# An attention, routing and expert kernel: the last 768 tokens of the routing moved into six blocks

## The chip, the cores and the metric

The kernel runs on one core of one Trainium2 chip. The metric is the device time of one execution in microseconds (us), as the median of several runs. The profiled execution is one more run, with a trace of every engine.

## The reference

Three stages follow each other: an attention with local windows and block sums, a mixture of 8 experts with a greedy assignment, and a dense layer pair. The change lies in the second. Its reference, cut to what matters:

```python
def _moe_ref(x, w_gate, w1, w2):          # x: 1536 x 512, w1: 8 x 512 x 1024, w2: 8 x 1024 x 512
    cap = N // E                          # 192
    flat = (x @ w_gate).flatten()
    for idx in np.argsort(-flat):         # greatest logit first
        tok, e = idx // E, idx % E
        if assigned[tok] >= 0 or counts[e] >= cap:
            continue
        assigned[tok] = e
        counts[e] += 1
    for e in range(E):
        out[assigned == e] = np.maximum(x[assigned == e] @ w1[e], 0.0) @ w2[e]
```

The last stage is `h = x @ w_in; r = max(h, 0); out = (r * r) @ w_out`, with 2048 hidden columns.

## The kernel before

**Routing in phases.** The 1536 tokens stand as 12 blocks (NBLK) of 128 in the tile `L9`, 128 partitions by 12 blocks by 9: eight logits, and a ninth column that is a floor. One phase finds the expert that is full first, closes it and takes its 192 tokens out. A phase has these steps, all in `Route` and in `routing()` inside `moe`:

- `top` (L508) takes each token's greatest open logit `m`, `choice` (L514 to L522) its expert as a one-hot `o` (the tiles `O32`) and, on GpSimd, its complement `no`.
- `row` (L534, L537) turns `m` into one row of 1536 values on every partition: 12 transposes on TensorE, three copies on ScalarE. `quarters` (L554) lays a copy out for the comparison below.
- `ge` (L570) compares, on VectorE, the whole row with each block's `m`: twelve tiles `G` of 128 x 1536, bf16. `count` (L582) multiplies them with the one-hots on TensorE, 32 rows of the result at a time, four products of 384 columns for a block of tokens, and so gets each token's rank within its expert. `cand` (L591, L593) turns the ranks into the threshold.
- A transposition (L761) and a chain of small VectorE instructions give the expert `ei` and the threshold `th`. Two products with a triangle and with ones (L799, L800) number the selected tokens; L803 to L829 mark the dead ones in `L9`.
- `t_hot` (L847 to L853), `t_idx` (L861, one small product for a block), `t_spread` (L870) and `t_sum` (L879, L880, with the casts L888 to L893) make a list of the 192 token numbers; `t_gather` (L905, L907) lets GpSimd issue two indirect DMAs, `xa` and `xb`, that fetch their rows of x.

Phase 0 stands in the attention stage by a table of its own. Phases 1 to 7 run beside the experts.

**Experts.** `x_t` (L957, L959) transposes the gathered rows, `expert` (L976, L993) does 64 matmuls of 128x128 by 192 columns in float32 for each expert. Weights come through SyncE's queue (`w_load`, L945) into eight buffers, two experts' worth.

**What sets the order.** `routing()` and `expert()` are generators. A loop at the end of `moe` keeps a clock of estimates (`T.p`, `T.v`, `T.a` for TensorE, VectorE, ScalarE) and appends to the program, at each turn, whichever of routing, the transposes of a gather or the next expert matmul can start first by that clock. A `yield t` says that the step behind it is ready at t. The order of each engine is so fixed when the program is built, and an instruction whose input is late holds up all behind it on its engine. Matmuls of an expert fill TensorE between routing's steps. `conv_idle` puts steps of the last stage's weight conversion (L647 to L657, from tiles `raw`) where VectorE is idle by that clock.

Two lines decide where a phase's index list is made:

```python
late = ph > 3                      # L720: the list of phase ph - 1 is made after this phase's row
now = ph < 3 or ph >= E - 2        # L822: the list of phase ph is made at once
```

So the lists of phases 3 to 5 are made inside the next phase.

**Last stage.** `hmm` (L1083) and `omm` (L1110) are float32r matmuls with 512 columns from about 312 us on.

Of the kernel before, what the change touches and what calls it, by code (L numbers as in the profile page):

```python
# [446 lines left out]
class Route:  # L447


    def __init__(self, tc, nc, L9, identf):  # L450
        self.tc, self.nc, self.L9, self.identf = tc, nc, L9, identf
        self.ctx = ExitStack()
        self.started, self.cnt, self.ng = set(), None, 0

    def open(self):
        nc, L9 = self.nc, self.L9
        rp = self.rp = self.ctx.enter_context(self.tc.tile_pool(name="m_r", bufs=1, side="right", reuse_waits="tile"))
        ii = rp.tile([128, 128], I32, name="ii")
        fi = rp.tile([128, 128], F32, name="fi")
# [4 lines left out]
        ji = rp.tile([128, 128], I32, name="ii")  # L464
# [33 lines left out]
    def new(self, ph):  # L498
        rp = self.rp
        self.m = rp.tile([128, NBLK], F32, name="m", bufs=2)  # L500
        self.eq = rp.tile([128, NBLK, E + 1], F32, name="eq")
        self.mw = rp.tile([128, NBLK], F32, name="mw")
        self.no = rp.tile([128, NBLK, E], F32, name="no")
        self.o = self.O32[ph % 2]

    def top(self, b0=0, b1=NBLK):

        self.nc.vector.reduce_max(self.m[:, b0:b1], self.L9[:, b0:b1], axis=AX.X)  # L508

    def choice(self, b0=0, b1=NBLK, onehot=True):  # L510

        nc, b = self.nc, slice(b0, b1)
# [36 lines left out]
    def quarters(self, b0, b1):  # L549
        nc = self.nc  # L550
        for g in range(b0 // 3, (b1 + 2) // 3):
# [25 lines left out]
    def count(self, pieces, last=False):  # L577

        for n, (c, j0, j1, t) in enumerate(pieces):
            for g in range(j0 // 3, (j1 + 2) // 3):  # L580
                lo, hi = max(j0, 3 * g), min(j1, 3 * g + 3)
                self.nc.tensor.matmul(self.cnt[32 * g:32 * g + 32, 128 * (lo - 3 * g):128 * (hi - 3 * g)],  # L582
                                      self.o[:, c, :], t[:, 128 * (lo - j0):128 * (hi - j0)],
# [4 lines left out]
    def cand(self):  # L588

        nc = self.nc  # L590
        nc.vector.scalar_tensor_tensor(self.mg, self.cnt, -(CAP - 0.5) * CS, self.mg, op0=OP.add, op1=OP.min)  # L591
        self.tm = self.rp.tile([128, 1], F32, name="tm")
        nc.vector.reduce_max(self.tm, self.mg, axis=AX.X)  # L593


def moe(tc, nc, R0, x_dram, m_dram, L9, w1, w2, win, wout, out, identf, identb, dbg=None):
# [101 lines left out]
    def routing():  # L698
        tm_at = T.v(0.1)
        for ph in range(E):  # L700
            d = st[ph] = {}
            ei = rp.tile([128, 8], U32, name="ei", bufs=4)
            es = rp.tile([128, 1], F32, name="es")
            if ph > 0:
                R0.new(ph)
                R0.top()
                m_at = T.v(0.33)
# [11 lines left out]
            if 0 < ph < E - 1:  # L719
                late = ph > 3  # L720
# [3 lines left out]
                R0.row(0, NBLK, ms4)  # L724
                row_at = T.a(1.6, T.p(1.3, m_at))
# [5 lines left out]
                G = R0.ge(0, NBLK)  # L731
                pend, ats = [], []

                def more(n):
                    while len(ats) < min(n, NBLK):
                        pend.extend(next(G))
                        ats.append(T.v(1.0, row_at))

                more(1)
                R0.quarters(0, NBLK)  # L740
# [6 lines left out]
                more(NG)  # L747
                c = 0
                for n in (2,) * 6 if ph == 1 else (4,) * 3:
                    c += n  # L750
                    yield ats[c - 1] + 0.1
                    R0.count(pend[c - n:c], c == NBLK)
                    T.p(0.3 + 0.165 * n, ats[c - 1] + 0.1)
# [32 lines left out]
            os_ = rp.tile([128, NBLK], F32, name="os")  # L786
            nc.vector.tensor_scalar(os_, mw, es, None, op0=OP.is_equal)
            sel = rp.tile([128, 2, NBLK], BF, name="sel")
# [10 lines left out]
            nc.tensor.matmul(ps[:, 0:24], low, s2, start=True, stop=True, skip_group_check=True)  # L799
            nc.tensor.matmul(ps[:, 24:48], ones, s2, start=True, stop=True, skip_group_check=True)  # L800
            T.p(0.07, sel_at + 0.1)
            sc = rp.tile([128, 24], F32, name="sc")
            nc.vector.tensor_tensor_scan(sc, ps[:, 24:48], zero24, 0.0, op0=OP.add, op1=OP.add)  # L803
# [384 lines left out]
```

## Time and profile before

| | us |
|---|---|
| median of 3 runs (580.49 to 580.98) | 580.73 |
| profiled execution, whole | 581.22 |
| its span, first to last instruction | 579.0 |
| TensorE (PE) busy in the span | 565.8 |
| VectorE (DVE) busy | 343.7 |
| ScalarE (ACT) busy | 197.0 |
| GpSimd (POOL) busy | 78.6 |

The page gives each engine's busy time, the span in 40 slices, the queues, the chain of work that ended last and the costliest groups of instructions. The views of the trace go closer: windows give busy times of a stretch, the chain gives pieces in order of time with what each added, the timeline gives each engine's instructions with start and duration, waits say who waited for whom. A duration is that of one instruction from start to its end; neighbours on an engine overlap, so a price in a stream is the distance between starts. A float32 matmul has two records.

### The profile page before, as it was taken

To read this page: it belongs to the slowest core of one execution; us is meant where nothing else is said; L and a number is where in the kernel's file an instruction comes from. 1 tells how busy PE (TensorE), PEld (TensorE's weight loads), DVE (VectorE), ACT (ScalarE), POOL (GpSimd) and SP (SyncE) were. 2 spreads that over 40 slices of the span, in tenths; PEclk is the share of its full clock that TensorE was granted. 3 is DMA by queue.
4 is the path that set the end of the run, shared out by engine and by line. 5 is a ranking of instruction groups with operands and counts; after the bars stand their busy time and mean duration, and the time that the engine had idled before them with its cause. 6 is when DMAs were issued, how large, how long until landed. Compare 5 with 4: busy or idle time off the path is not lost.

```text
span 579.0 us, 10522 instructions
## 1 busy us (share of the span) xinstructions
PE 565.8 (98%) x4131; PEld 473.7 (82%) x4131; DVE 343.7 (59%) x773; ACT 197.0 (34%) x421; POOL 78.6 (14%) x136
## 2 busy tenths in 40 slices
PE   6999998999999999999999999999999999999995
PEld 4778873698998989899999888888888888888884
DVE  6885688877879688765664987833222223222222
ACT  4887871331413313132232433423212213212221
POOL 6564400210202042020000000000300000300002
PEclk9999999999999999999999999999999999999998
DMA  9997223646544545869742443400100000100001
GB/s 225 244 198 148 93 76 121 227 144 219 199 173 143 196 143 203 291 220 402 248 157 84 145 146 109 146 0 2 72 2 0 1 0 1 72 1 0 1 0 72
DMA packets 55392, 71.33 MB, mean 123 GB/s; under 512 B 21296, under 2 KB 32560, under 8 KB 55344
## 3 DMA queue, kind: packets, MB, share of 16 engines
q1 hardware_dynamic: 53360, 64.38, 35.6%
q0 software_dynamic: 1984, 6.29, 3.2%
q8 instruction: 32, 0.52, 0.4%
q14 instruction: 16, 0.13, 0.1%
HBM read 64.37 MB, written 6.29 MB: 122 GB/s over the span
## 4 chain that ended last, share of the span: by engine, by line
PE 78%; issue 14%; DVE 3%; DMA 2%; POOL 1%; SPq 1%; ACT 1%; POOLq 0%; DVEq 0%; ACTq 0%
PE pg L1083 16%; PE ph L976 15%; PE ph L993 15%; PE ph L1110 11%; PE px L1110 4%; PE O L284 2%; PE cnt L582 2%; PE T L270 2%; DMA rawq<-in_q_dram 2%; DVE G L570 2%; PE S L250 2%; POOL out_dram L1123 1%; PE ms L534 1%; PE T L193 1%; PE T L321 1%
## 5 line engine op out<-in xcount | busy, mean ns | idle before, releaser
L976 PE MATMUL ph<-xt,w 128*128 128x192 f32 x512 | 90.6, 330 | 0.0
L570 DVE TENSOR_SCALAR G<-mrow,m 128x1536 bf16<-128x1536 f32 (+4 forms) x108 | 84.7, 837 | 8.1 <-ACT mrow L537 4.8
L993 PE MATMUL ph<-ht,w 128*128 128x192 f32 x512 | 89.3, 329 | 0.0
L993 PEld LDWEIGHTS ph<-ht,w 128*128 128x128 f32 x512 | 82.9, 190 | 2.9 <-issue 2.5
L976 PEld LDWEIGHTS ph<-xt,w 128*128 128x128 f32 x512 | 82.5, 190 | 2.8 <-issue 2.1
L1083 PE MATMUL pg<-yhi,w 128*128 128x512 f32 x192 | 59.1, 389 | 0.0
L1087 DVE TENSOR_TENSOR xa<-xa 128x512 f32<-128x512 f32 x24 | 16.6, 691 | 60.1 <-ACT xa L1086 60.0
L1087 DVE TENSOR_TENSOR xb<-xb 128x512 f32<-128x512 f32 x24 | 16.6, 691 | 59.6 <-ACT xb L1086 59.6
L1123 POOL DMA_INDIRECT out_dram<-f,sci x6 | 5.9, 978 | 300.7 <-DVE f L1121 300.0
L1083 PEld LDWEIGHTS pg<-yhi,w 128*128 128x128 f32 x192 | 36.0, 188 | 7.5
L981 ACT ACTIVATE ht<-ph 128x384 f32<-128x384 f32 x32 | 15.7, 490 | 65.3 <-PE ph L976 61.6
L1083 PE MATMUL pg<-ylo,w 128*128 128x512 f32 x96 | 37.3, 389 | 0.0
L1086 ACT ACTIVATE xb<-pg 128x512 f32<-128x512 f32 x24 | 14.3, 596 | 65.7 <-PE pg L1083 65.7
L1086 ACT ACTIVATE xa<-pg 128x512 f32<-128x512 f32 x24 | 14.3, 596 | 63.5 <-PE pg L1083 63.5
L1110 PE MATMUL ph<-w,xt 128*128 128x512 f32 x144 | 35.2, 389 | 0.0
L1110 PEld LDWEIGHTS ph<-w,xt 128*128 128x128 f32 x144 | 27.0, 188 | 5.6
L1083 PE MATMUL pg<-yhi,w2a 128*128 128x512 f32 x96 | 29.7, 391 | 0.0
L1083 PE MATMUL pg<-yhi,w2b 128*128 128x512 f32 x96 | 29.6, 389 | 0.0
L999 ACT ACTIVATE yhi<-ph 128x384 fp32r<-128x384 f32 x16 | 7.8, 491 | 58.4 <-PE ph L993 58.4
L263 ACT ACTIVATE P<-S,nm 128x120 f32<-128x120 f32 x96 | 26.6, 373 | 2.3 <-DVE nm L259 2.2
L905 POOL DMA_INDIRECT xa<-x_dram,sci x8 | 10.8, 1356 | 87.2 <-DVE sci L893 65.3
L1083 PEld LDWEIGHTS pg<-yhi,w2b 128*128 128x128 f32 x96 | 18.0, 188 | 3.8
(245 smaller groups left out, 982.4 us busy)
## 6 DMA issues: line engine op xcount, KB each, us to landing
w<-in_moe_w_dram SPq DMA_DIRECT2D x64, 512.0 KB, 6.1
raw<-in_moe_w_in_dram SPq DMA_DIRECT2D x14, 512.0 KB, 3.8
raw<-in_moe_w_out_dram SPq DMA_DIRECT2D x14, 512.0 KB, 3.3
vw<-in_v_dram SPq DMA_DIRECT2D x16, 240.0 KB, 6.7
rawk<-in_k_dram SPq DMA_DIRECT2D x8, 384.0 KB, 5.8
rawq<-in_q_dram SPq DMA_DIRECT2D x8, 384.0 KB, 7.1
x_dram<-x SPq DMA_DIRECT2D x10, 256.0 KB, 2.0
w<-in_moe_w_in_dram SPq DMA_DIRECT2D x2, 512.0 KB
```

What stands on the lines that cost most here:

```text
L250: nc.tensor.matmul(ss[hh][64 * par:64 * par + 64, i, :], QT[b, hp][r, 128 * c + 64 * par:128 * c + 64 * par + 64], KW_[b, hp][r, 2 * c + p ...
L263: nc.scalar.activation(P[u][:, hh, i], SS[u][hh][:, i], AF.Exp, bias=NM[u][:, hh, i:i + 1])
L270: nc.tensor.transpose(ps[0:KW, i, :], P[u][:, hh, i, :], identf)
L570: self.nc.vector.tensor_scalar(t[:, used:used + w], self.mrow[:, 128 * j0:128 * j1], self.m[:, c:c + 1], CS, op0=OP.is_le, op1=OP.mult)
L976: nc.tensor.matmul(ps[:, j, 0:CAP], w[:, k, 128 * (f % 4):128 * (f % 4) + 128], d["xt"][:, k, :], start=(k == 0), stop=(k == 3), skip_grou ...
L981: nc.scalar.activation(d["ht"][:, f0:f0 + 2, :], ps[:, :, 0:CAP], AF.Relu)
L993: nc.tensor.matmul(ps[:, j, 0:CAP], w[:, f % 4, 128 * dd:128 * dd + 128], d["ht"][:, f, :], start=(f == 0), stop=(f == 7), skip_group_chec ...
L1083: nc.tensor.matmul(ps, a[:, k, fs], b[:, k, js], start=(n == 0), stop=(n == 11))
L1086: nc.scalar.activation(r, ps, AF.Relu)
L1087: nc.vector.tensor_tensor(r, r, r, op=OP.mult)
L1110: nc.tensor.matmul(PO[j][t], a[:, 128 * t:128 * t + 128], b[:, f % 4, :], start=(f == 0 and n == 0), stop=(f == 15 and n == 2))
L1123: sc = nc.gpsimd.indirect_dma_start(out=out, out_offset=bass.IndirectOffsetOnAxis(ap=sci[:, 4 * j + t:4 * j + t + 1], axis=0), in_=o, in_o ...
```

## The change

After phase 3 four experts are full and half of the tokens, 768, are left. A new generator, `halve`, then moves these into six blocks. It marks the tokens that are still alive, numbers them with the triangle and the ones as L799 and L800 do, and splits that number into a block (six of them) and a place in the block (128). The logits and the token number of each token are split into three bf16 parts that add up to them exactly (27 values). For each of the 12 old blocks a 128x128 matrix of zeros and ones says which place a token goes to, and one matmul with 6 x 27 = 162 columns carries the 27 values there; the twelve add up in PSUM. Two reductions add the three parts into the new `L9`, six blocks wide, and the new token numbers. From then on `nb` is 6 in place of 12: the row has 768 columns in 6 transposes, there are 6 tiles `G` of 128 x 768, the counts have 24 products of 192 columns in one batch, and the index lists take 6 products. `late` becomes `ph > 4` and `now` becomes `ph < 4 or ph >= E - 2`, so the list of phase 3 is made at once. `open` makes two new constants on GpSimd, and uses parts of the tile `mrow` as scratch.

The diff, cut to its core:

```diff
@@ Route.open
+        self.io7 = rp.tile([128, 128], BF, name="io7")
+        self.c128 = rp.tile([128, NBLK // 2], I32, name="c128")
...
+        scratch = rp.tile([128, N], F32, name="mrow")
+        ii, ji = [scratch[:, c:c + 128].bitcast(I32) for c in (0, 256)]
+        fi = scratch[:, 128:256]
+        nc.gpsimd.iota(self.c128, pattern=[[128, NBLK // 2]], base=2048, channel_multiplier=0)
...
+        nc.gpsimd.tensor_scalar(self.io7, fi, 1.0, -1.0, op0=OP.mult, op1=OP.add)
@@ Route.count
+        w = 32 * self.nb
         for n, (c, j0, j1, t) in enumerate(pieces):
-            for g in range(j0 // 3, (j1 + 2) // 3):
-                lo, hi = max(j0, 3 * g), min(j1, 3 * g + 3)
...
+            for g in range(128 * j0 // w, (128 * j1 + w - 1) // w):
+                lo, hi = max(128 * j0, w * g), min(128 * j1, w * g + w)
...
+    def halve(self, tiles):
...
+        nc.vector.reduce_max(self.m, L9[:, :, 0:E], axis=AX.X)
+        nc.vector.tensor_scalar(alive, self.m, -BIG / 4, None, op0=OP.is_gt)
+        yield 0.4
+        ps = tiles()
+        nc.tensor.matmul(ps[:, 0:NBLK], self.low, alive, start=True, stop=True, skip_group_check=True)
+        nc.tensor.matmul(ps[:, NBLK:2 * NBLK], self.ones, alive, start=True, stop=True, skip_group_check=True)
+        nc.vector.tensor_copy(parts[:, :, 0:9], L9)
+        nc.vector.tensor_tensor(rest, L9, parts[:, :, 0:9], op=OP.subtract)
...
+        nc.vector.tensor_copy(parts[:, :, 9:18], rest)
...
+        nc.vector.tensor_tensor(parts[:, :, 18:27], rest, parts[:, :, 9:18], op=OP.subtract)
+        nc.gpsimd.memset(L9[:, :, E:E + 1], -BIG / 2)
...
+        nc.vector.tensor_tensor(own, hi[:, :, None].to_broadcast([128, NBLK, NBLK // 2]),
+                                self.c128[:, None, :].to_broadcast([128, NBLK, NBLK // 2]), op=OP.is_equal)
+        yield 1.9
...
+        for h in range(2):
+            b = slice(6 * h, 6 * h + 6)
+            nc.vector.tensor_tensor(mine[h], parts[:, b, None, :].to_broadcast([128, 6, 6, 27]),
+                                    own[:, b, :, None].to_broadcast([128, 6, 6, 27]), op=OP.mult)
+            for c in range(6 * h, 6 * h + 6):
+                nc.vector.tensor_scalar(hot[:, c, :], self.io7, low7[:, c:c + 1], None, op0=OP.is_equal)
+        yield 3.6
+        for c in range(NBLK):
+            nc.tensor.matmul(sums, hot[:, c, :], mine[c // 6][:, c % 6].rearrange("p a b -> p (a b)"),
+                             start=c == 0, stop=c == NBLK - 1)
+        self.nb = NBLK // 2
+        self.L9 = L9[:, 0:self.nb]
+        got = sums.rearrange("p (t a e) -> p t e a", t=self.nb, a=3)
+        nc.vector.reduce_sum(self.L9[:, :, 0:E], got[:, :, 0:E], axis=AX.X)
+        tok = self.rp.tile([128, NBLK], F32, name="ua")[:, 0:self.nb]
+        nc.vector.reduce_sum(tok, got[:, :, E, :], axis=AX.X)
+        nc.gpsimd.tensor_copy(self.tok[:, 0:self.nb], tok)
+        yield 0.5
@@ routing
+            if ph == 4:
+                half = R0.halve(lambda: p_s.tile([128, 162], F32, name="ms", bufs=3))
+                at = T.v(next(half)) + 0.1
+                yield max(at, st[ph - 1]["hs_at"])
+                t_sum(ph - 1)
...
+                yield at
+                next(half)
...
-                late = ph > 3
+                late = ph > 4
...
-                for n in (2,) * 6 if ph == 1 else (4,) * 3:
+                for n in (2,) * 6 if ph == 1 else (4,) * 3 if nb == NBLK else (nb,):
...
-            now = ph < 3 or ph >= E - 2
+            now = ph < 4 or ph >= E - 2
...
+                if ph == 3:
+                    nc.gpsimd.tensor_copy(L9[:, :, E:E + 1], R0.tok[:, :, None])
```

The other edits cut the same tiles and constants to `nb` blocks and scale the clock's estimates with `nb`.

How the order moves, at the places that the prediction speaks of. First TensorE from phase 3's selection on, before; `ph<-xt` and `ph<-ht` are an expert's first and second layer, `ms<-identf,m` the row transposes of phase 4, `ms<-hot,ohi` the index products of phase 3:

```order
L800 MATMUL ms<-sel,ones 128x24
L976 MATMUL ph<-xt,w_2646 128x192 x9
L534 MATMUL ms<-identf,m 128x128 x12
L976 MATMUL ph<-xt,w_2646 128x192 x3
...
L861 MATMUL ms<-hot,ohi 32x16
L976 MATMUL ph<-xt,w_2646 128x192 x4
L993 MATMUL ph<-ht,w_2658 128x192
...
L880 MATMUL ms<-one_1053,hs 64x1
...
L582 MATMUL cnt<-G,O_0_1065 32x384
```

And the same stretch now, where `ms<-G` are the twelve products of the new step:

```order
L886 MATMUL ms<-sel,ones 128x24
...
L970 MATMUL ms<-one_1056,hs 64x1
L627 LDWEIGHTS low
L627 MATMUL ms<-sel,low 128x12
...
L628 MATMUL ms<-sel,ones 128x12
...
L656 MATMUL ms<-G 128x162
...
L1047 MATMUL px<-identf,xa 128x128 x2
...
L541 MATMUL ms<-identf,m 128x128 x6
...
L596 MATMUL cnt<-G,O_0_1068 32x192
```

The index list of phase 3 is finished ahead of phase 4's row, the two numbering products of the new step stand right behind `t_sum(3)`, and the row transposes of phase 4 come behind the twelve products and behind the transposes of gather 3.

VectorE's queue for the new step, now; the `G` tiles are its work space, `io` the row 0 to 127, `c` the six block numbers:

```order
L624 TENSOR_SCALAR sel<-m 128x12
L978 CAST sci<-ms 128x1
L979 CAST ib<-ms 64x1
L983 CAST sci<-ms 64x1
L629 CAST G<-L_67 128x12x9
...
L643 TENSOR_TENSOR G<-hi,c_1034 128x72
L650 TENSOR_TENSOR G<-G 128x972
L653 TENSOR_SCALAR G<-io_1033,G 128x128 x6
L719 TENSOR_SCALAR f<-raw 128x512
L661 TENSOR_REDUCE L_67<-ms 128x6x8
```

All of it is new but the three casts and the conversion step L719; it stands between the casts of gather 3 and the first instruction of phase 4.

## Rows read from the trace of the kernel before

**Rows 1.** Windows: stretch; PE, PEld, DVE, ACT, POOL busy (records); clock; DMA share, GB/s.
```profile
170.00:260.00 90.00, 90.00 (x723) 80.76 (x721) 71.45 (x199) 25.81 (x52) 16.15 (x19) 1.00 0.58 199
312.00:570.00 258.00, 258.00 (x1138) 213.34 (x1138) 107.68 (x170) 72.28 (x120) 10.29 (x17) 1.00 0.12 40
```

**Rows 2.** Waits of TensorE, 100 to 260 us: total, times, longest.
```profile
PE cnt L582 <- DVE G L570: 0.3, 1, 0.3
PE ms L879 <- DVE hs L870: 0.2, 1, 0.2
```

**Rows 3.** Chain from 96 to 312 us: start, us, what, records.
```profile
173.27 1.31 PE ms L534 x12
...
175.56 0.17 PE ms L861 x12
...
181.12 0.76 PE cnt L582 x16
181.89 3.45 PE ph L993 x20
...
186.10 0.37 PE px L957 x2
...
199.54 0.98 PE ph L976 x6
...
253.65 0.22 PE px L957 x2
...
258.75 10.40 PE ph L993 x64
...
311.77 0.46 PE pg L1083 x2
```

**Rows 4.** Timeline of TensorE late in phase 0: start, duration, instruction.
```profile
88.68 0.62 PE L582 MATMUL S<-G,O 128*32 128x128 bf16 x16
89.23 0.82 PE L368 MATMUL T<-identb 128*128 128x512 bf16 x3
89.99 1.05 PE L582 MATMUL S<-G,O 128*32 128x384 bf16 x13
```

**Rows 5.** Timeline of TensorE and its weight loads at 170 us.
```profile
170.04 0.18 PE L799 MATMUL ms<-sel,low 128*128 128x24 bf16 x1
170.04 0.10 PEld L800 LDWEIGHTS <-ones 128*128 128x128 bf16 x1
170.07 0.17 PE L800 MATMUL ms<-sel,ones 128*128 128x24 bf16 x1
```

**Rows 6.** Timeline of VectorE, at 84 and 149 us.
```profile
84.30 0.87 DVE L570 TENSOR_SCALAR G<-mrow,m 128x256 bf16<-128x256 f32 x3
...
148.66 0.26 DVE L508 TENSOR_REDUCE m<-L 128x12 f32<-128x108 f32 x1
...
149.64 0.16 DVE L888 CAST sci<-ms 128x1 int32<-128x1 f32 x1 [0.41 <-PE ms L880]
```

**Rows 7.** The page's groups: busy, mean ns of one, idle before.
```profile
L1087 DVE TENSOR_TENSOR xa<-xa 128x512 f32<-128x512 f32 x24 | 16.6, 691 | 60.1 <-ACT xa L1086 60.0
```

**Rows 8.** Timeline of GpSimd: the gathers of phases 3 and 4.
```profile
178.15 1.12 POOL L905 DMA_INDIRECT xa<-x_dram,sci  x1 [4.03 <-DVE ib L889]
179.57 1.54 POOL L907 DMA_INDIRECT xb<-x_dram,ib  x1 [0.30 <-issue]
...
203.11 3.52 POOL L905 DMA_INDIRECT xa<-x_dram,sci  x1 [4.03 <-DVE ib L889]
206.93 1.54 POOL L907 DMA_INDIRECT xb<-x_dram,ib  x1 [0.30 <-PE cnt L582]
```

**Rows 9.** Timeline of SyncE's queue: expert 6's third weight block.
```profile
255.29 0.99 SPq L945 DMA_DIRECT2D w<-in_moe_w_dram  x2
```

**Rows 10.** DMA issues, 177 to 188 and 255 to 272 us: us to landing.
```profile
xb<-x_dram,ib POOLq DMA_INDIRECT x1, 3.6
...
xb<-x_dram,ib POOLq DMA_INDIRECT x1, 6.4
```

More of the change, by code (lines that the diff above doesn't have):

```diff
@@ L452, in __init__ @@
         self.ctx = ExitStack()
-        self.started, self.cnt, self.ng = set(), None, 0
+        self.started, self.cnt, self.ng, self.nb = set(), None, 0, NBLK
     def open(self):
@@ L550, in quarters @@
         nc = self.nc
+        if self.nb < NBLK:
+            w = 32 * self.nb
+            for g in range(4):
+                nc.scalar.activation(self.mg[32 * g:32 * g + 32, 0:w], self.mrow[32 * g:32 * g + 32, w * g:w * g + w],
+                                     AF.Copy)
+            return
         for g in range(b0 // 3, (b1 + 2) // 3):
@@ L703, in routing @@
             es = rp.tile([128, 1], F32, name="es")
+            if ph == 4:
[3 more added lines that the diff above has]
+                t_sum(ph - 1)
+                T.p(0.2)
+                at = T.v(next(half), T.pe + 0.2)
+                at = T.v(next(half)) + 0.1
+                yield at
+                next(half)
+                T.p(1.2)
+                T.v(0.5, T.pe + 0.2)
+            nb = R0.nb
+            L9 = R0.L9
             if ph > 0:
@@ L706, in routing @@
                 R0.top()
-                m_at = T.v(0.33)
+                m_at = T.v(0.1 + 0.02 * nb)
                 pick = R0.choice(onehot=ph < E - 1)
@@ L723, in routing @@
                 yield m_at + 0.1
-                R0.row(0, NBLK, ms4)
-                row_at = T.a(1.6, T.p(1.3, m_at))
+                R0.row(0, nb, ms4)
+                row_at = T.a(0.13 * nb, T.p(0.11 * nb, m_at))
                 if late:
@@ L798, in routing @@
             ps = p_s.tile([128, 48], F32, name="ms", bufs=3)
[L799 to L800 removed]
+            nc.tensor.matmul(ps[:, 0:2 * nb], low, s2, start=True, stop=True, skip_group_check=True)
+            nc.tensor.matmul(ps[:, 24:24 + 2 * nb], ones, s2, start=True, stop=True, skip_group_check=True)
             T.p(0.07, sel_at + 0.1)
[L802 to L803 removed]
+            sc = rp.tile([128, 24], F32, name="sc")[:, 0:2 * nb]
+            nc.vector.tensor_tensor_scan(sc, ps[:, 24:24 + 2 * nb], zero24[:, 0:2 * nb], 0.0, op0=OP.add, op1=OP.add)
             if ph < E - 1:
[L805 removed]
+                a = rp.tile([128, NBLK], F32, name="ua")[:, 0:nb]
                 nc.vector.tensor_scalar(a, m, th, None, op0=OP.is_gt)
[L807 removed]
+            nc.vector.tensor_tensor(sc, ps[:, 0:2 * nb], sc, op=OP.add)
             if ph < E - 1:
@@ L858, in t_idx @@
         ps = d["px"] = p_s.tile([128, 16], F32, name="ms", bufs=3)
-        for c in range(NBLK):
+        nb = d["hot"].shape[1]
+        for c in range(nb):
             g = slice(32 * (c % 4), 32 * (c % 4) + 32)
-            nc.tensor.matmul(ps[g, :], R0.ohi[:, c, :], d["hot"][:, c, :], start=c < 4, stop=c >= 8,
+            nc.tensor.matmul(ps[g, :], R0.ohi[:, c, :], d["hot"][:, c, :], start=c < 4, stop=c + 4 >= nb,
                              skip_group_check=True)
```

111 lines of the change are left out of this document (67 added, 44 removed).

## The prediction

> **What bounds the kernel now.** I read the windows by stage first. From 170 to 260 us, where routing phases 4 to 6 and the experts share the engines, TensorE is busy for the whole 90 us, at a granted clock of 1.00, which is the 2.4 GHz level, and again from 312 to 570 us [rows 1]. VectorE is busy for 71 of the 90 us and the DMA engines for 0.58 of them. A busy TensorE need not be one at its peak, so the waits come next: between 100 and 260 us TensorE waited twice, 0.5 us in all [rows 2], and from 305 us on the same view has no row at all. So the time from about 110 us on is the sum of what stands in TensorE's queue, and the chain of waits gives each piece a price [rows 3]. An expert's matmul (128x128 by 192 columns, float32, two records each) costs 0.325 us: 64 records of L993 in 10.40 us.
>
> One price hides in that chain. 20 records of L993 right behind a count batch took 3.45 us, where 10 matmuls at 0.325 us are 3.25 us; 6 records right behind the float32 transposes of L534 took 0.98 us, the bare 3 x 0.325. And the first transposes of L957 took 0.37 us behind a count batch and 0.22 us behind float32 work [rows 3]. So every return from a 16-bit group to float32 costs 0.2 us before an expert's matmul and 0.15 us before a transpose. Batches have a price of their own, beside their columns.
>
> **What is removed from TensorE.** In phases 4, 5 and 6 (the fifth to seventh):
> - Counts. Before, 9 batches of 16 products with 384 columns, 0.76 us each [rows 3], 6.9 us. Now 3 batches of 24 products with 192 columns. The four products of a piece run in four column groups of the array at once: a quartet of 384 took 191 ns, of which 384 columns at 2.4 GHz are 160 ns, so 31 ns are not columns. Half the columns make 80 + 31 = 111 ns, six quartets 0.67 us, three phases 2.0 us. The 16 products with 128 columns in phase 0, between 88.68 and 89.23 us [rows 4], two groups at a time, are 69 ns a pair: 53 ns of columns and 16 ns more, the same 8 ns for each product. Ends: 14 ns each, as L861's twelve products in 0.17 us [rows 3], give 0.34 us a phase; no gain for fewer columns (48 ns each) gives 1.15 us. Saved: 4.9 us (3.4 to 5.9).
> - Row transposes. 12 in 1.31 us [rows 3], 109 ns each; 6 fewer in three phases save 2.0 us.
> - Index products (L861). 6 fewer in each of phases 4 to 7 at 14 ns save 0.3 us.
> - Returns to float32. Nine count batches become three, and one batch of the new step is added. Before: 6 x 0.2 + 3 x 0.15 (three were followed by the transposes of a gather) = 1.65 us. Now 3 x 0.2 + 0.15, and some 0.1 us where transposes now stand behind a selection: 0.85 us. Saved: 0.8 us (0 to 1.2).
>
> **What is added to TensorE.** Two products with 12 columns, right behind the two of t_sum(3): the pair L799, L800 starts 0.03 us apart [rows 5], so 0.05 us. And 12 products with 162 bf16 columns, each with its own 128x128 weights: no row has this shape. The nearest is the 512-column bf16 product with 128x128 weights, three between 89.23 and 89.99 us [rows 4], 253 ns each, 213 ns of it columns, 40 ns more. 162 columns are 67.5 ns, so about 0.1 us each and 1.2 us in all. Ends: the columns alone, 0.8 us; a weight load of 0.10 us [rows 5] in front of each and hidden by nothing, 2.4 us. I take 1.2 us, because in rows 5 the product of L800 starts 0.03 us after its own load began, so loads do hide. [...]
>
> TensorE's sum: -4.9 - 2.0 - 0.3 - 0.8 + 0.05 + 1.2 = -6.75 us (-3.5 to -8.4).
>
> **What the new step asks of VectorE, and who waits.** TensorE's order is fixed in advance, so a late VectorE makes it stand, and the experts' matmuls behind it stand too. From the end of t_sum(3) TensorE has 19 expert matmuls ahead of the first 128x162 product: 6.2 us and one return, 6.4 us. VectorE meanwhile does three casts for the gather (0.16 us each, partly on top of each other [rows 6]; 0.3 us, an estimate), then eleven small instructions. A reduction over 108 elements lasts 0.26 us [rows 6]; several of the eleven have 12 elements, so I take 0.2 us each, 2.3 us. Then two products of 972 bf16 elements: 512 float32 elements take 0.69 us [rows 7], so at most 1.3 us; I take 1.2 us. Then 12 comparisons over 128 elements: three of 256 elements of L570 took 0.87 us in a row [rows 6], so under 0.29 us; I take 0.2 us. The order is product, 6 comparisons, product, 6 comparisons, and each TensorE product waits for its own comparison alone. The first six are there at 0.3 + 2.3 + 1.2 + 1.2 = 5.0 us, ahead of TensorE; the last at 7.4 us, and TensorE undisturbed would come to it at 6.4 + 1.1 = 7.5 us. So nothing waits, by a hair: I charge 0.2 us, up to 2 us. Next VectorE adds up the new logits (0.3 us), the token numbers and the new maxima while TensorE does the transposes of gather 3, 0.8 us: again level.
>
> GpSimd gets five small instructions, two of them ahead of a reader: the copy of the token numbers into L9 stands in front of gather 3's issue, and the fill of L9's ninth column stands behind that issue; its reader, the new maximum, comes over 8 us after t_sum(3), where the two issues take 3.0 to 5.4 us [rows 8]. Nothing is charged. The start-up instructions that open() now has more of run at 46 to 50 us, long before any reader, and cost nothing. VectorE loses 36 comparisons of 1536 elements and gains 18 of 768; nobody waited for it, so this is worth nothing by itself.
>
> **SyncE.** Two raw loads of the last stage now stand ahead of expert 6's third weight block, which before was issued at 255.29 us [rows 9]. That weight's first use comes after expert 5's second layer (258.75 us) and expert 6's first, over 20 us later; a hold-up of some microseconds is covered. The gather of phase 3 is issued 3 us earlier, since t_hot(3) no longer waits for phase 4's transposes.
>
> **The gathers.** Between t_sum(p) and the transposes of gather p there were 8.4 us; now, for p = 4 and 5, 20 expert matmuls (6.5 us), one count batch (0.7 us), 0.15 us of small products and two returns: 7.7 us, and 7.6 us for p = 3. Casts and the way to GpSimd take 0.4 us of it. Gather 3 needed 179.57 - 178.15 + 3.6 = 5.0 us after its issue began; gather 4 needed 3.8 us to the second issue and some 3.5 us, 7.3 us [rows 8, 10]. 7.3 us are left, so at worst a touch at one of them. I charge 0.05 us.
>
> **Sum.** -6.75 + 0.25 = -6.5 us. The profiled execution took 581.22 us (span 579.0), 0.5 us above the median of the runs, so 574.7 us for a profiled one and 580.73 - 6.5 = **574.2 us** for the median.
>
> **Rivals.**
> 1. VectorE's chain is late: comparisons at 0.29 us and products at 1.3 us, eleven small ones at 0.29 us. The last product then comes at 9.6 us, and TensorE waits 2 us: 576.3 us. For it: the margin worked out above is nearly nil. Against it: most of the eleven have few elements. 10 in 100.
> 2. Prices on TensorE don't fall with columns (count products at 48 ns) and the twelve loads don't hide: 1.4 + 1.2 us less gain, 576.8 us. 10 in 100.
> 3. The other side, slower: every gather takes the worst of both, 3.8 us to the second issue and 6.4 us to landing, as gather 7 did under full DMA load [rows 10], 10.2 us against 7.3 us. TensorE stands 2.9 us three times, 8.7 us: 582.9 us. It makes the kernel slower once the mean gather is over 9.6 us after its issue. For it: gather 4's first issue took 3.52 us instead of 1.12 us [rows 8] and the new bf16 work runs on VectorE during gather 3. [...] 8 in 100, half of it slower than before, the rest 576 to 582 us.
> 4. It doesn't do what it says: the experts' weights or another stream set the pace as soon as TensorE gets quicker, and the 6.5 us come back as waits: 580.7 us. Against it: no row shows TensorE waiting for a weight. 6 in 100.
>
> **Chances and range.** The forecast has 66 in 100. Faster by over 0.2% (1.2 us, about what a measurement here can tell) 0.88, within 0.2% 0.06, slower 0.06. The range takes in rivals 1 and 2 and the low end of TensorE's sum: 572.8 to 577.4 us.
>
> **What would show it.** In the profile after: L976, L993 and the counts still without a gap; count batches of 24 in 0.67 us, three of them; 12 products 128x162 in about 1.2 us from about 181 us; the first L1083-type matmul of the last stage near 305.3 us instead of 311.77 us [rows 3]; the last stage unchanged. Waits of TensorE for a comparison over 128 elements mean rival 1, for xa or xb rival 3, for a weight rival 4. The prediction is wrong if TensorE shows over 2 us of new waits between 170 and 310 us.

## The result and the profile after

The changed kernel took 573.61 us (median of 4 runs, 573.49 to 574.59) against 580.86 us before in the same session: a ratio of 0.9879, 95% interval 0.9862 to 0.9896. The forecast was 574.2 us. Its profiled execution has a span of 571.8 us, 7.2 us under the one before.

The windows by stage come first, with the columns of [rows 1]. The last stage now runs from 304 to 565.5 us.

```profile
170.00:260.00 90.00, 89.75 (x664) 84.98 (x663) 60.46 (x222) 24.10 (x54) 12.93 (x21) 1.00 0.76 267
305.00:563.00 258.00, 258.00 (x1139) 213.53 (x1138) 105.03 (x166) 71.46 (x118) 10.73 (x18) 1.00 0.11 38
```

TensorE is still full where [rows 1] showed it full, and VectorE has lost 11 of 71 us, which is worth nothing by itself (the fourth experiment). TensorE's waits from 100 to 260 us, which answer to [rows 2], have one new row, 0.2 us for the second half of gather 5:

```profile
PE cnt L596 <- DVE G L583: 0.3, 1, 0.3
PE px L1049 <- DMA xb<-x_dram,ib: 0.2, 1, 0.2
PE ms L969 <- DVE hs L960: 0.2, 1, 0.2
```

The chain of waits around the new step answers to [rows 3] (start, us, what, records; L627 and L628 are the numbering pair, L656 the 12 products of 162 columns, L541 the row transposes, L596 the counts, L951 the index products, L1173 the last stage):

```profile
173.24 0.12 PE ms L970
173.37 0.11 PE ms L627
173.48 0.03 PE ms L628
173.50 2.05 PE ph L1066 x12
175.56 4.23 PE ph L1083 x26
179.78 0.86 PE ms L656 x12
180.64 0.22 PE px L1047 x2
...
181.47 0.80 PE ms L541 x6
182.27 4.88 PE ph L1083 x30
187.15 0.61 PE cnt L596 x24
187.75 1.50 PE ph L1083 x8
...
195.35 0.66 PE ms L541 x6
...
197.63 0.14 PE ms L951 x6
...
202.19 0.61 PE cnt L596 x24
...
209.42 0.65 PE ms L541 x6
...
304.12 8.21 PE pg L1173 x36
```

The marks that the prediction set are there, some with other sizes: counts in one batch of 0.61 us (0.67 forecast; the third batch, from 215.87 us, lies beside this chain, which follows the gather there), 12 products in 0.86 us (about 1.2 forecast), one short wait, and the last stage at 304.12 us (305.3 forecast), 7.65 us sooner than the 311.77 us of [rows 3]. Six row transposes take 0.66 us in two phases, and 0.80 us in phase 4, where they stand behind the transposes of a gather.

Not all of the 7.65 us belongs to the change. The clearest yardstick is TensorE's time from its first transposition of tm (in routing phase 0) to its last group of matmuls, since what lies ahead of it varies from one execution to the next. Before, from 95.86 to 572.31 us, it is 476.45 us:

```profile
95.86 0.29 PE L761 MATMUL ms<-identf,tm 128*128 128x128 f32 x1 [0.44 <-DVE tm L593]
...
572.31 0.84 PE L1110 MATMUL px<-w,ht 128*128 128x512 f32 x3
```

After, from 95.13 to 564.66 us,

```profile
95.13 0.29 PE L847 MATMUL ms<-identf,tm 128*128 128x128 f32 x1 [0.44 <-DVE tm L608]
...
564.66 0.84 PE L1200 MATMUL px<-w,ht 128*128 128x512 f32 x3
```

it is 469.53 us. **On TensorE the change is worth 6.92 us.** The other 0.73 us are the earlier start at tm. The first load on the chain also landed sooner, 7.09 us after its issue where before it took 10.21 us; that the one makes the other is not shown (experiments 8 and 11).

### The profile page after: what moved, and what is told of

It is laid out like the page before. It is cut to its first block, busy times and chain, and to the rows that moved or that the text cites. A ratio compares the mean times of both kernels' runs of the same rounds, so it can differ in the third digit from the quotient of the medians.

```text
span 571.8 us, 10320 instructions
## 1 busy us (share of the span) xinstructions
PE 559.1 (98%) x4031; PEld 471.9 (83%) x4031; DVE 321.5 (56%) x784; ACT 192.9 (34%) x418; POOL 78.0 (14%) x141
## 4 chain that ended last, share of the span: by engine, by line
PE 77%; issue 14%; DVE 3%; DMA 2%; POOL 2%; ACT 0%; SPq 0%; POOLq 0%; DVEq 0%; ACTq 0%
PE pg L1173 16%; PE ph L1083 15%; PE ph L1066 14%; PE ph L1200 11%; PE px L1200 4%; PE O L284 2%; PE S L250 2%; PE T L270 2%; DVE G L583 2%; PE T L193 1%; PE cnt L596 1%; POOL out_dram L1213 1%; DMA rawq<-in_q_dram 1%; DMA xb<-x_dram,ib 1%; PE T L321 1%
## 5 line engine op out<-in xcount | busy, mean ns | idle before, releaser
L583 DVE TENSOR_SCALAR G<-mrow,m 128x1536 bf16<-128x1536 f32 (+4 forms) x90 | 60.0, 722 | 4.9 <-ACT mrow L544 4.4
L1173 PE MATMUL pg<-yhi,w 128*128 128x512 f32 x192 | 59.2, 389 | 0.0
L1173 PEld LDWEIGHTS pg<-yhi,w 128*128 128x128 f32 x192 | 36.1, 188 | 7.5
L1173 PE MATMUL pg<-ylo,w 128*128 128x512 f32 x96 | 37.4, 389 | 0.0
L1173 PE MATMUL pg<-yhi,w2a 128*128 128x512 f32 x96 | 29.7, 391 | 0.0
L1173 PE MATMUL pg<-yhi,w2b 128*128 128x512 f32 x96 | 29.6, 390 | 0.0
L1173 PEld LDWEIGHTS pg<-yhi,w2b 128*128 128x128 f32 x96 | 18.0, 188 | 3.7
```

Of the source, the lines that this page charges most:

```text
L583: self.nc.vector.tensor_scalar(t[:, used:used + w], self.mrow[:, 128 * j0:128 * j1], self.m[:, c:c + 1], CS, op0=OP.is_le, op1=OP.mult)
L1173: nc.tensor.matmul(ps, a[:, k, fs], b[:, k, js], start=(n == 0), stop=(n == 11))
```

## The experiments

"TensorE's stretch" below is that yardstick, 476.45 us before and 469.53 us after. The lines of the code carry the numbers of the kernel that the experiment started from, before or after; an added line shifts those in the profile by a few.

**1. What does a batch cost?** The kernel before, with small batches in all phases:

```
-                for n in (2,) * 6 if ph == 1 else (4,) * 3:
+                for n in (2,) * 6:
```

> The kernel before, with the counts of phases 2 to 6 in six batches of two columns instead of three batches of four: the same 48 count products of 384 columns in a phase, but 5 x 3 = 15 more batches among the expert's matmuls. It puts a price on the batch itself. My theory, that each return from a 16-bit group to float32 costs 0.2 us before an expert's matmul: 15 x 0.2 = 3.0 us slower, 583.3 to 584 us, and the bare 384-column quartet stays at 191 ns. The rival, that the returns cost nothing and the saved 0.8 us came from elsewhere: 580.8 us, no change within 0.5 us.

Measured: 591.76 us, with one run of the four at 584.25 us and three from 591.2 to 592.7 us; ratio 1.0156 (1.0081 to 1.0230). The 583.3 to 584 us that were expected did not come. Most of the excess is neither the batch nor the return. In the profiled run TensorE stood 5.0 us for a gather (waits, then GpSimd's timeline and VectorE's, start and duration in us):

```profile
PE px L957 <- DMA xa<-x_dram,sci: 5.0, 1, 5.0
```
```profile
200.33 10.03 POOL L905 DMA_INDIRECT xa<-x_dram,sci  x1 [4.03 <-DVE ib L889]
```
```profile
200.03 0.14 DVE L893 CAST sci<-ms 64x1 int32<-64x1 f32 x1
200.10 9.37 DVE L570 TENSOR_SCALAR G<-mrow,m 128x1536 bf16<-128x1536 f32 x10
```

GpSimd's issue lasts from 200.33 to 210.36 us. VectorE's ten comparisons, without a pause, end at 209.47 us, 0.89 us earlier, and in the kernel before an issue with no comparison beside it took 0.90 to 1.16 us (248.97 and 101.99 us). So by its timing the issue got through only when the run was over. In the kernel before VectorE has to pause for a free tile G (0.67 us, for the counts), since three large batches return tiles late: the 3.52 us issue of [rows 8] (203.11 to 206.63 us) ends 0.89 us after three comparisons, at 205.74 us. With small batches the tiles come back in time and the run never breaks.

After the stand the granted clock was low for some microseconds (windows, columns as above), and the same pieces took longer, the counts 0.76 instead of 0.44 us and the transposes 0.69 instead of 0.37 us:

```profile
205.00:210.00 5.00, 2.93 (x28) 1.84 (x26) 4.47 (x5) 0.10 (x1) 5.00 (x1) 1.00 0.01 3
210.00:215.00 5.00, 2.06 (x16) 1.36 (x16) 0.00 (x0) 0.49 (x2) 1.35 (x3) 0.56 0.47 124
215.00:220.00 5.00, 5.00 (x34) 4.08 (x27) 1.11 (x2) 0.88 (x3) 0.00 (x0) 0.76 0.95 342
```

The batch itself, in a stretch of this run at clock 1.00:

```profile
230.89 0.44 PE cnt L582 x8
231.33 1.82 PE ph L976 x10
233.16 0.44 PE cnt L582 x8
233.59 2.15 PE ph L976 x12
```

Five and six expert matmuls are 1.625 and 1.95 us; both groups took 0.2 us more. So the return to float32 costs what the prediction says behind a count batch. But the theory missed a second fixed price: 8 products take 0.44 us, 16 take 0.76 us, so 0.32 us for 8 products more, which is 160 ns a quartet of 384 columns, 0.42 ns a column, and 0.12 us for each batch. 15 more batches then cost 15 x 0.32 = 4.8 us. TensorE's stretch is 488.29 us, 11.84 us more: 4.8 + 5.0 of standing + 2.1 us which the rows right behind the stand took longer than the same pieces at full clock.

**2. Is the earlier gather worth something?** The kernel before, with the list of phase 3 made at once:

```
-                if ph < 4 or ph == E - 1:
+                if ph < 5 or ph == E - 1:
...
-                late = ph > 3
+                late = ph > 4
...
-            now = ph < 3 or ph >= E - 2
+            now = ph < 4 or ph >= E - 2
```

> The kernel before, with the token list of phase 3 made at once, ahead of the next phase's transposes, as the changed kernel has it: the gather of phase 3 is issued about 3 us earlier, and nothing is left out or added. My theory, TensorE's queue being full, says that an earlier gather is worth nothing by itself: 580.8 us, within 0.5 us. The rival, that part of the 7.2 us gained comes from the earlier list and gather and not from shorter work on TensorE: faster by 1 us or more.

Measured: 581.28 us, ratio 1.0016 (1.0005 to 1.0027), TensorE's stretch 477.00 us. Gather 3 is issued 3.8 us earlier than in [rows 8]:

```profile
174.37 1.00 POOL L905 DMA_INDIRECT xa<-x_dram,sci  x1 [21.49 <-DVE sci L893]
```

and it buys nothing: the kernel is 0.6 us slower, with a new wait of 0.2 us for ht (L993). None of the gain comes from there.

**3. Are the transposes on the path?** The changed kernel, with the row transposes of phases 4 to 6 twice:

```
+                for _ in range(2 if self.nb < NBLK else 1):
-                nc.tensor.transpose(ps[:, c, :], ...)
+                    nc.tensor.transpose(ps[:, c, :], ...)
```

> The changed kernel, with the six row transposes (L541) of each of phases 4 to 6 issued twice into the same place: 18 more float32 transposes on TensorE, and VectorE's comparisons 0.65 us later in each phase. My theory, the time is the sum of TensorE's queue: 18 x 0.109 us = 1.96 us slower than the changed kernel, 575.6 us. The rival, that routing has slack on TensorE after the change and the transposes taken away were not what gained: 573.6 us, no change.

The clock of estimates was told of the longer row, so what follows is placed accordingly.

Measured: 575.91 us, ratio to before 0.9914 (0.9897 to 0.9930); TensorE's stretch 471.61 us, 2.1 us more than after, where 18 x 0.109 = 1.96 us were expected. A transpose added costs what a transpose taken away was said to save.

**4. Is VectorE's relief worth something?** The changed kernel, each comparison of phases 4 to 6 twice:

```
-            self.nc.vector.tensor_scalar(t[:, used:used + w], ...)
+            for _ in range(2 if self.nb < NBLK else 1):
+                self.nc.vector.tensor_scalar(t[:, used:used + w], ...)
```

> The changed kernel, with each of the 18 comparisons of phases 4 to 6 (L583) issued twice on VectorE, which gives back the VectorE time that the change took away there: about 18 x 0.53 us = 9.6 us more work on VectorE. My theory, VectorE's relief is worth nothing because TensorE has 20 expert matmuls to do meanwhile: 573.6 us, up to 0.3 us more. The rival, that the gain comes from a shorter chain of routing on VectorE: a good part of 3 x 3.2 us back, 577 to 583 us.

The clock of estimates was told of the longer comparisons too (a line not shown), so the counts stand later in TensorE's queue, behind more expert matmuls.

Measured: 573.37 us, ratio to before 0.9872 (0.9856 to 0.9888), TensorE's stretch 469.09 us. VectorE's windows show the work back, and TensorE, with its queue ordered for it, lost nothing:

```profile
170.00:260.00 90.00, 90.00 (x667) 85.51 (x666) 68.43 (x235) 23.66 (x53) 11.75 (x21) 1.00 0.73 256
```

68.43 us of VectorE against 60.46 us after. TensorE has one wait less, even, the 0.2 us at L1049.

**5. How near was VectorE to being late?** The changed kernel, with the two large products of the new step twice:

```
+            for _ in range(2):
-            nc.vector.tensor_tensor(mine[h], ...)
+                nc.vector.tensor_tensor(mine[h], ...)
```

> The changed kernel, with the two VectorE products of 972 elements in the new step (L650) issued twice, TensorE's order unchanged: 2.2 us more on VectorE ahead of the last of the 12 products. The trace after shows the last comparison ending about 0.3 us ahead of the last of the 12 products, so my theory (hidden by a hair) expects TensorE to stand 2.2 - 0.3 = 1.9 us there: 575.5 us. The rival, that VectorE's chain had several microseconds of room: 573.6 us.

Measured: 577.43 us (576.02 to 579.04), ratio to before 0.9950 (0.9934 to 0.9966). The waits say 1.7 us, near the 1.9 expected; the windows behind them say the rest:

```profile
PE ms L657 <- DVE G L654: 1.7, 1, 1.7
```
```profile
184.00:188.00 4.00, 4.00 (x21) 3.23 (x22) 2.54 (x13) 1.14 (x3) 0.42 (x2) 0.57 1.01 375
188.00:192.00 4.00, 4.00 (x27) 4.00 (x26) 3.36 (x7) 2.54 (x7) 0.00 (x0) 1.00 0.38 145
```

At clock 0.57 two groups of gather 3's transposes took 0.43 us each, which take 0.22 us each in after, and 4 us hold what 2.3 us would at 1.00 (an estimate, 4 x 0.57). So the stand of 1.7 us cost about 3.4 us here. In the profiled execution, the slowest, the clock was also low once at 95 us (0.66 from 95 to 100 us), far ahead of the edit: the way from tm to a count of phase 1 that VectorE releases in both kernels (108.90 us in after) took 15.30 us instead of 13.77 us. 1.7 + 1.7 + 1.5 is the 4.9 us by which TensorE's stretch (474.47 us) grew. The run at 576.02 us had a mean clock of 0.998, the median run 0.994: it may be that the clock does not fall after every such stand, but neither run has a trace.

**6. Is it only the place in the queue?** The same, with the 12 products placed later:

```
-        yield 3.6
+        yield 5.9
```

> As the one before, but the 12 products of TensorE are placed 2.3 us later in its queue, behind 7 more expert matmuls. My theory, that the wait comes only from the place in the queue: back to the changed kernel, 573.6 us, up to 0.5 us more. The rival, that the later step delays the next selection and gather and TensorE stands there instead: 575 us or more.

Measured: 573.57 us, ratio to before 0.9889 (0.9872 to 0.9905), TensorE's stretch 469.36 us, no wait at the new step and none for a gather. In the trace it is not 7 more expert matmuls that stand ahead of the 12 products but 4, and the transposes of gather 3; the products begin 8.4 us after the numbering pair instead of 6.3 us. The 2.2 us of VectorE's work cost nothing as soon as TensorE's queue has other work to do meanwhile.

**7 and 10. Two steps.** The same idea once more: 1152 tokens are moved into nine blocks before phase 2, and 768 into six before phase 4.

```
+STEPS = {2: 9, 4: 6}
...
-    def halve(self, tiles):
+    def halve(self, tiles, new):
...
-            if ph == 4:
+            if ph in STEPS:
...
-                for n in (2,) * 6 if ph == 1 else (4,) * 3 if nb == NBLK else (nb,):
+                for n in (2,) * 6 if ph == 1 else {12: (4, 4, 4), 9: (4, 5)}.get(nb, (nb,)):
```

> The changed kernel, with the remaining tokens moved together twice: the 1152 left before phase 2 into nine blocks, and the 768 left before phase 4 into six as now. Exact 0/1 products in both. Phases 2 and 3 have 9 row transposes instead of 12, nine comparisons, and two count batches (of 4 and 5 columns with 288 wide) instead of three. Working from the rows of the trace after: counts 2 x 1.0 us less, transposes 6 x 0.109 = 0.65 us less, two returns 0.4 us less, the second step over nine columns 0.2 us less; the first step costs 12 products of 243 columns, 12 x 0.105 = 1.27 us, a numbering pair 0.14 us and a return 0.2 us. Sum -1.65 us against the changed kernel: 572.0 us (571.5 to 573). The rival, that the early phases' gathers and VectorE's step are not hidden: TensorE stands there, 573.6 us or more.

Measured: 572.18 us, ratio to before 0.9870 (0.9853 to 0.9888), TensorE's stretch 468.02 us, with no wait for a gather. Beside the changed kernel once more:

> The kernel with the two steps once more, beside the changed kernel in the same call, since their intervals still overlapped. My theory, from the queue of TensorE: 1.5 us under the changed kernel, ratio of the two 0.9974. The rival, that the earlier difference was an earlier start of TensorE in that profile: no difference within 0.5 us.

Measured: 572.24 us (571.30 to 572.43), ratio to before 0.9840 (0.9821 to 0.9860), stretch 467.75 us. Against after's 469.5 us that is 1.5 and 1.7 us, where 1.65 us were expected. By the medians of the two sessions the gain over the changed kernel is 1.5 and 1.9 us; the intervals of the ratios overlap in the first (0.9853 to 0.9888 and 0.9874 to 0.9908) and just part in the second (0.9821 to 0.9860 and 0.9864 to 0.9920), and the traces agree with them. One term of the expected sum is not there: behind the first step's 12 products 8 records of an expert take 1.31 us, the bare 1.30 us, and no return of 0.2 us. The chain of waits of the second execution gives three more prices (L659 the products, now 12 with 243 columns and 9 with 162; L598 the counts with 288 columns):

```profile
133.08 1.27 PE ms L659 x12
...
141.20 0.60 PE cnt L598 x16
...
144.93 0.73 PE cnt L598 x20
...
179.07 0.65 PE ms L659 x9
```

**8 and 11. What varies by itself?** The changed kernel, unedited, twice more.

> The changed kernel once more, as it is. Two pieces of the difference between the two traces were in no step of the prediction: the first load landed 3.1 us sooner after its issue (7.09 instead of 10.21 us) and TensorE's start followed by 0.7 us, and the last scatter's landing took 0.45 us more. My theory is that both vary from execution to execution and are no part of the change: here they differ from the first trace's values while the ratio stays at 0.988 to 0.989. The rival, that they belong to the changed kernel: the same 7.1 us and 4.2 us again.

Measured: 573.67 us, ratio 0.9891 (0.9874 to 0.9908), stretch 469.48 us. The first load took 7.29 us after its issue, TensorE's tm came at 95.35 us. Over all the profiles that point lies between 94.0 and 96.0 us, and the two kernels built on before that changed nothing ahead of it had it at 93.99 and 95.33 us: the early start is no part of the change. The first load does not set that point alone: in experiment 11 it took 10.39 us, with tm at 95.73 us, and in experiment 9 6.54 us, with tm at 95.64 us. The end is another matter: from the start of the last scatter's issue to the end of the span are 4.7 us in before, in its three variants and in the kernels with two steps, and 5.1 us in all three profiles of after and in its four variants. 0.4 us thus belong to the changed program. What causes them was not tried.

> The changed kernel as it is, beside the kernel with two steps. My theory: 573.4 to 573.8 us, 6.4 to 7.2 us under the kernel before, and 469.5 us from the first transposition of tm in routing to TensorE's last matmul, as in both its profiles. The rival, that chips differ by more than that: 1 us off.

Measured: 574.17 us (572.58 to 576.98), 0.4 us above what was expected, but 6.6 us under before, as expected; ratio 0.9892 (0.9864 to 0.9920), stretch 469.45 us. Two of its six runs were at 576.9 us with a mean clock of 0.994; they were not profiled and their cause is open.

**9. Does the unbroken run hold up the issue?** The first experiment with three tiles G instead of five:

```
-                    t = self.rp.tile([128, N], BF, name="G", bufs=5)
+                    t = self.rp.tile([128, N], BF, name="G", bufs=3)
...
-    NG = 5
+    NG = 3
```

> The first experiment (the kernel before with six count batches in each of phases 1 to 6), now with a ring of 3 tiles G instead of 5, so that VectorE must pause for TensorE after at most three comparisons. In the first experiment one gather's first issue on GpSimd lasted 10.03 us, under an unbroken run of ten comparisons of 9.37 us, and ended 0.89 us after that run; TensorE then stood 5.0 us, and three of its four runs were at 591 to 593 us, one at 584.25 us. My theory, that an issue can be held up as long as VectorE's run of comparisons is unbroken: with the short ring no issue over 3.5 us, no stand for xa or xb over 0.5 us, and all runs at 584 to 586 us. The rival, that the long issue came from the descriptors or the DMA queues and not from VectorE: issues up to 10 us and times of 590 us again.

Measured: 587.58 us (586.41 to 590.10), ratio to before 1.0124 (1.0096 to 1.0152). In the profiled run, at 586.41 us, VectorE pauses after one comparison and the longest issue of all is (VectorE's row, then GpSimd's)

```profile
202.38 1.00 DVE L570 TENSOR_SCALAR G<-mrow,m 128x1536 bf16<-128x1536 f32 x1
203.63 1.95 DVE L570 TENSOR_SCALAR G<-mrow,m 128x1536 bf16<-128x1536 f32 x2 [0.26 <-PE cnt L582]
```
```profile
202.60 2.17 POOL L905 DMA_INDIRECT xa<-x_dram,sci  x1 [4.03 <-DVE ib L889]
```

with no wait for xa or xb. So what was expected of the issue and the stand holds in this one profile, and with the stand the low clock went too (1.00 in all windows from 60 to 305 us). The times missed: the other three runs lie 0.8 to 3.7 us higher, at lower mean clocks, and none of them has a profile, so whether a longer issue came back in them is open. TensorE's stretch is 481.82 us, 5.37 us above before; 0.9 us of it is a new wait for ht, and the 4.5 us left are 0.30 us for each of the 15 batches, near the corrected price of experiment 1 (0.12 + 0.2). An issue also got through before the end of an unbroken run in experiments 5 and 6, with five tiles (1.56 us each, beside four comparisons of 2.19 us), so the short ring by itself does not prove what holds an issue up.

**12. Larger batches in phase 1 too.** The kernel with two steps, with three batches of four:

```
-                for n in (2,) * 6 if ph == 1 else {12: (4, 4, 4), 9: (4, 5)}.get(nb, (nb,)):
+                for n in {12: (4, 4, 4), 9: (4, 5)}.get(nb, (nb,)):
```

> The kernel with two steps, and the counts of phase 1 in three batches of four columns instead of six of two. My theory: each batch left out saves its fixed 0.12 us and the return of 0.2 us, 3 x 0.32 = 0.96 us, so 571.2 us where the two steps take 572.2. The rival, that TensorE has little else to do in phase 1 and stands longer for the fourth comparison: no gain, 572.2 us or more.

Measured: 571.87 us (571.06 to 573.51), ratio to before 0.9847 (0.9821 to 0.9872), stretch 467.40 us: 0.35 us less than experiment 10 had. Most of the 0.96 us is not there. In the chain its first batch starts at 107.26 us, behind filler matmuls of 4.10 us (L768, which only keep TensorE busy): phase 1 begins with TensorE ahead of its work, which would explain why a price taken off TensorE there takes little off the time. That was not tried further.

## Why the prediction was right

Its steps against the rows, in us saved (+) or added (-) on TensorE:

| step | predicted | measured | from |
|---|---|---|---|
| counts, phases 4 to 6 | +4.9 | +5.0 | 9 x 0.76 less 3 x 0.61 |
| row transposes | +2.0 | +1.8 | 3 x 1.31 less 0.80, 0.66 and 0.65 |
| index products | +0.3 | +0.12 | 0.17 less 0.14, four times |
| returns to float32 | +0.8 | +1.2 | the experts' matmuls 0.87 us less, the gathers' transposes 0.03 us less with 0.3 us of waiting in them |
| numbering pair | -0.05 | -0.14 | 0.11 + 0.03 |
| 12 products with 162 columns | -1.2 | -0.86 | L656 x12 |
| waits | -0.25 | -0.3 | L1049 |
| sum | +6.5 | +6.8 | stretch: +6.92 |

The prices are counted as in the chain, from the end of one group of matmuls to the end of the next (so the wait of 0.2 us comes to 0.3 us). The largest term, the counts, was sized rightly. The others miss by up to 0.4 us, in both directions, and that they cancel is luck. So is the match of the waits: the 0.2 us were charged to VectorE's chain, which kept nobody waiting, and came from a gather, which was charged 0.05 us. The ends that the prediction gives for TensorE's sum, -3.5 and -8.4 us, come to -3.3 and -8.6 us when its terms are added; nothing hangs on it.

- **What bounds the kernel** was read rightly. Experiments 2 and 4 give or take GpSimd's and VectorE's time and nothing moves; experiment 3 puts 18 transposes on TensorE and the time follows by what they cost there.
- **Counts: the sum was right, its law was not.** The prediction put 31 ns on every quartet beside its columns. The batches show that a quartet costs its columns alone, and a batch 0.12 us once: 0.12 + 4 x 0.16 = 0.76 (384 columns), 0.12 + 4 x 0.12 = 0.60 (288), 0.12 + 6 x 0.08 = 0.60 (192, measured 0.61). The 16 products with 128 columns of [rows 4], 0.55 us, are 0.12 + 8 x 0.053 us. For one batch of six quartets both laws give nearly the same, 0.67 and 0.60 us; for experiment 1 they differ by 1.8 us, and there the theory failed.
- **Returns: the price was right behind count batches, the law was not.** The prediction puts the 0.2 us on the step from 16-bit work back to float32, and took the float32 transposes of L534 as its proof. The transposes of a gather are float32 too, and the expert matmuls right behind them pay 0.2 us, in the kernel before already (14 records, 7 x 0.325 = 2.28 us bare):

```profile
186.95 0.12 PE ms L959 x2
187.07 2.47 PE ph L993 x14
```

Nor do all 16-bit groups charge it. Behind the 12 new products the transposes of gather 3 take 0.22 us (180.64 us), as behind float32 work, where the prediction charged 0.15 us; behind a numbering pair the excess is 0.1 us. What the groups behind which 0.14 to 0.2 us are lost have in common in the timeline is that they use a part of the array (counts and index products 128\*32, L970 128\*64, L1049 64\*128), while the numbering pairs, the 12 products and the row transposes use all of it (128\*128). No run tests this by itself.

- **The new products were priced too high.** 72 ns each, 67.5 ns of them columns. With experiment 10 (106 ns at 243 columns, 72 ns for nine at 162) the law is the columns, 0.42 ns each (34 ns for 81 more), and some 0.05 us for the group. That is 2.4 columns in a ns at clock 1.00, and it is as much as the runs show of the 2.4 GHz by which the prediction counts columns: the trace gives the clock as a share alone. A quartet of counts takes the same 0.42 ns for each column of one of its four products (experiment 1), so the four do run at once. The 40 ns above its columns that [rows 4] shows for the 512-column product did not carry over. A load of L656 took 98 ns (the mean of 12 in after); with 67.5 ns of columns behind it that would be 166 ns a product if nothing hid it. The products come every 72 ns, so the loads are hidden, and the upper end of 2.4 us was far off.
- **Index products** were priced by the piece, 14 ns; a group of 12 takes 0.17 us and one of 6 takes 0.14 us. Most of it is a price for the group.
- **VectorE "by a hair"** was right in size. The eleven small instructions ran one into the other, from 173.83 to 176.05 us; the comparisons came every 0.16 us where 0.2 us were charged:

```profile
176.05 1.17 DVE L650 TENSOR_TENSOR G<-G 128x972 bf16<-128x972 bf16 x1
177.14 1.06 DVE L653 TENSOR_SCALAR G<-io,G 128x128 bf16<-128x128 bf16 x6
178.11 1.16 DVE L650 TENSOR_TENSOR G<-G 128x972 bf16<-128x972 bf16 x1
179.19 1.06 DVE L653 TENSOR_SCALAR G<-io,G 128x128 bf16<-128x128 bf16 x6
```

The last comparison ends at about 180.2 us, the last of TensorE's 12 products starts at about 180.55 us: 0.3 us of room, and the 0.2 us charged for it was not needed. What rival 1 would have cost was too low, though: experiment 5 shows that a stand of 1.7 us cost 3.4 us, clock included, where the prediction counted the stand alone.

- **Gathers (rival 3).** It did not come true, but a first issue held up as in [rows 8] is there again. By its timing the 3.52 us issue was already held up by VectorE: it ends 0.89 us after three comparisons (experiment 1). In the changed kernel the issue of gather 4 took 2.85 us, and it ends 0.89 us after VectorE's four comparisons (199.31 to 201.50 us):

```profile
199.31 2.19 DVE L583 TENSOR_SCALAR G<-mrow,m 128x768 bf16<-128x768 f32 x4
```
```profile
199.54 2.85 POOL L995 DMA_INDIRECT xa<-x_dram,sci  x1 [3.56 <-DVE ib L979]
...
213.29 1.25 POOL L995 DMA_INDIRECT xa<-x_dram,sci  x1 [3.22 <-DVE ib L979]
214.84 0.91 POOL L997 DMA_INDIRECT xb<-x_dram,ib  x1 [0.30 <-issue]
```

Gather 5 had the fast issue but 6.3 us to landing, which is the 0.2 us that TensorE stood. Halving the comparisons also shortens the run that can hold an issue up (2.19 us here, 2.86 us before), which the prediction did not see as a point in the change's favour.

- **Median.** In the three sessions the changed kernel is 7.25, 6.4 and 6.6 us under before; predicted 6.5 us. What the medians have beyond the stretch, in either direction, is the start, which varies by up to 2 us between executions, and the 0.4 us at the end.

## What to carry to other kernels

Where one engine's queue is full, price what a change takes out of that queue: columns at the full rate (0.42 ns each for bf16 at clock 1.00, four count products side by side counted once), plus a fixed price for each group of small 16-bit products (0.05 to 0.12 us) and 0.15 to 0.2 us for the float32 work right behind a group such as a count batch, and give nothing for relief on the other engines as long as the full one does not wait for them. Where a fixed order makes the full engine wait for a step, place the step behind enough other work: the same 2.2 us on VectorE cost 3.8 us in one place and nothing where the step stands some 2 us later. Before anything is changed that lets VectorE run on without a pause, look at how long the GpSimd issues beside it take (10.03 us beside a run of 9.37 us in experiment 1).

## What was not expected of the hardware

- **By their timing, indirect DMA issues on GpSimd can be held up by an unbroken run of VectorE's comparisons, up to its end.** 10.03 us under a run of 9.37 us (experiment 1), 3.52 us under 2.86 us (before), 2.85 us under 2.19 us (after), each ending 0.89 us after the run. It is not so each time. First issues of a gather (xa) that started within 0.03 us of the run's first comparison took 1.00 to 1.25 us, one of them under a run of ten; those that started 0.23 us into it were held to its end in before, after and experiments 1, 3, 7 and 8 (2.85 to 10.03 us), while in experiments 4, 5, 6 and 9 they took 1.26, 1.56, 1.56 and 2.17 us. Second issues (xb), which start later in a run, need not be held to its end: in experiment 1 one began 1.44 us into a run of ten and took 1.54 us. What decides is open. In experiment 1 the hold-up went on over ten instructions in a row; what it is in VectorE's run that holds the issue is not shown.
- **A short stand can cost twice.** After 5.0 us of standing (experiment 1) the granted clock was 0.56 and 0.76 in the two windows of 5 us at its end and behind it, after 1.7 us (experiment 5) it was 0.57 over 4 us; after 0.9 us (experiment 9) and 0.2 us (after) it stayed at 1.00.
- **A group of small products has a price as a group**, not by the piece: six index products 0.14 us, nine 0.16 us (experiment 7), twelve 0.17 us.
- **A count batch makes the float32 group behind it dearer, and so does a float32 transposition of 64 rows**, by 0.14 to 0.2 us each: 0.37 instead of 0.22 us for a gather's transposes and 3.45 instead of 3.25 us for ten expert matmuls behind the counts [rows 3], 2.47 instead of 2.28 us for seven behind L959, 0.80 instead of 0.66 us for six row transposes behind L1049. Behind the new 128\*128 products there is none of it, 0.22 us (180.64 us).
